# Where four small streams stand in a hand-ordered attention and gate kernel: key-feature exponentials, feature minima, LN2 norms, a memory product

## The chip, the cores and the metric

The kernel runs on one core of a Trainium2 chip. A core has TensorE (matmuls; PE in the profile, its weight loads PEld), VectorE (DVE), ScalarE (ACT), GpSimd (POOL) and SyncE (SP, which here only issues DMAs). Each engine executes its own instructions strictly in the order in which the program issued them, and waits at an instruction until what that needs is there. The metric is the time of one execution on the device, in microseconds; the median of several executions is compared.

## The reference, cut to what matters

A block of 2048 tokens of width 448 goes through attention with a compressive memory and then through a gated layer, each behind a layer norm that is modulated by a vector `c`:

```
mod = silu(c) @ w_mod -> sa, ca, ga, sb, cb, gb
h = LN(x) * (1 + ca) + sa
x = x + ga * attention(h)
h = LN(x) * (1 + cb) + sb
x = x + gb * ((sigmoid(h @ w_gate) * (h @ w_up)) @ w_down)

attention, for each of 4 segments of 512 tokens, 16 heads of width 28:
  phi(t) = t + 1 where t > 0, else exp(t)
  a_dot = softmax(causal(q k^T * scale)) v
  a_mem = (phi(q) M) / (phi(q) z + 1e-6)
  o     = g * a_mem + (1 - g) * a_dot        # g = sigmoid(beta)
  M, z  = M + phi(k)^T v, z + sum(phi(k))
```

So segment s reads a memory that the keys and values of the segments before it have filled; segment 0 reads an empty one.

## The kernel before

**Tiling.** Tokens are cut into 4 segments (s) of 4 tiles of 128. The 16 heads go in 4 chunks (hc) of 4 heads, each head padded from 28 to 32, so that a chunk fills 128 partitions. Attention is done one unit (s, hc) at a time. A unit has three groups g of key blocks (`KB_GROUPS`): block 0; blocks 1 and 3; block 2. I write (s, hc, g) for a group.

**One group** (`logits`, L405): TensorE makes the logits `lg` (L418) in the one PSUM tile for them, ScalarE takes exp into `pT` (L421), GpSimd masks the diagonal blocks (L429). At g = 0 of a later segment `phi` (L363) also starts the query features of the unit.

**`phi`** is an exponential on ScalarE (L365) and, some time later, a pair on VectorE: r = max(x, 0) + 1 (L369) and e = min(e, r) (L370), "the minimum" below. For keys (`mem_k`, L376) a DMA transpose, issued by SP, then brings e into `pk` (L380).

**Per unit besides:** `pv` (L432) multiplies `pT` with the values into `acc` (L443) and divides on VectorE (L449 to L456); `mem_read` (L460) multiplies the query features with the masked memory `rm` (L467) and divides (L470 to L474); `otr` (L485) transposes the unit's result by a DMA on SP (L490). They belong to the unit before the one whose logits are being made.

**Per segment:** `proj_qk` and `proj_v` (L338, L350) make queries, keys (cast by ScalarE or VectorE) and values (cast by ScalarE, L357); `mem_jobs` (L581) starts the four key features and does `mem_update` (L384): 16 matmuls into `dM` (L391), an addition on VectorE (L395, L397), the masking on GpSimd (L400). `wo_tile` (L505) is the output product of one token tile (L502), the addition to x (L512), the statistics of the second layer norm, LN2 (L269, L270), and its 1/std on GpSimd (`rstd`, L273, L274). Some time later `norm_t` (L283) normalizes the tile on VectorE (L277), copies a pad, and issues its DMA transpose into `hT` on SP (L287); when all four are there, `modulate` (L289, L291) scales each of the four chunks of `hT`. Then `gate_up` and `gate_up2` (L527, L546) make gate and up products for two blocks of 128 features (L534, L539, L551), tanh on ScalarE (L542) and the product `fT` on VectorE (L554); `down` (L556) makes one output tile from 14 blocks (L566), adds (L568) and stores it.

**PSUM.** All products but the logits rotate through four buffers (`ps_m`, tag "m"): a product waits until the one four before it has been read out.

**What sets the order.** The kernel issues its instructions in an order that a small planner in the code makes when the kernel is built. It has a clock (`clock`), advanced by `tick` with an assumed cost in ns of each job (a Q or K product 4 * 216, a V or output tile 4 * 190, a group of logits 450, a PV 1000, a memory read 250). `later(ns, fn, tag)` puts work off until the clock has passed its due time; `need(tag)` does all work of a tag at once. `fill` is a queue of jobs; after each group `run_fill` issues jobs for `pace` ns, and what it overran is carried as a (negative) `debt`. In segment 0 pace is 2400; from (s, 1, 0) on it is the cost of what is left, divided by 12. `gate_up2` is issued right behind the next group's logits. PV of the unit before stands in g = 1; where s > 1 it stands already in g = 0 if pace plus debt isn't positive.

The order of `fill` decides when a segment's other work is done. For segments 0 and 1 it is built at L749 to L754, for later ones at L780 to L801.

Of the kernel before, what the change touches and what calls it, by code (L numbers as in the profile page):

```python
# [17 lines left out]
def kernel(  # L18
# [16 lines left out]
    nc = tc.nc  # L35
# [11 lines left out]
    NHC = 4  # L47
# [328 lines left out]
    def mem_k(s, hc):  # L376
        if hc == 0:
            pk_of[s] = pipe.tile([P, NHC, TPS, P], BF16, tag="pk", bufs=1, name="pk")
        pk = pk_of[s]
        phi(kT_of[s][:, hc, :], 3500 if s < 2 else 5000, ("pk", s), lambda e: nc.sync.dma_start_transpose(pk[:, hc, :, :], e[:]))  # L380

    rm_of = {}

    def mem_update(s):  # L384
        need(("pk", s))
        pk = pk_of[s]
        dM = m_f32("dM")
        dMv = dM[:, 0:NHC * 4 * ME].rearrange("p (c h e) -> p c h e", h=4, e=ME)
        for hc in range(NHC):
            for kb in range(TPS):  # L390
                nc.tensor.matmul(dMv[:, hc, :, :], lhsT=pk[:, hc, kb, :],  # L391
                                 rhs=vt_all[s][:, kb, hc * 4:(hc + 1) * 4, 0:ME],
                                 start=(kb == 0), stop=(kb == TPS - 1))
        if s == 0:
            nc.vector.tensor_copy(M_sb[:], dMv)  # L395
        else:
            nc.vector.tensor_tensor(M_sb[:], M_sb[:], dMv, ALU.add)  # L397
        rm = pipe.tile([P, NHC, 4, ME], BF16, tag="rm", bufs=3, name="rm")
        rm_of[s + 1] = rm
        later(800, lambda: nc.gpsimd.tensor_tensor(rm[:], M_sb[:], bmask[:], ALU.mult), ("rm", s + 1))  # L400
# [4 lines left out]
    def logits(s, hc, g):  # L405
# [14 lines left out]
            wid += nq  # L420
        nc.scalar.activation(pT[:, :, w0:w0 + wid], lg[:, :, 0:wid], AF.Exp, scale=scale)  # L421
        if g == 0 and s > 0:
            pq_of[u] = phi(qT[:, hc, :], 3600, ("pq", u))
        for kb in KB_GROUPS[g]:
            later(2600, lambda kb=kb: mask(pT, kb), ("mask", u))

# [82 lines left out]
    def wo_fin(s, t):  # L509
        pw = pw_of.pop(t)  # L510
        xt = x_sb[:, s * TPS + t, :]
        nc.vector.tensor_tensor(xt, pw[:, 0:D], xt, ALU.add)  # L512
        if t == 0:
            ln2_of[s] = LN([x_sb[:, s * TPS + i, :] for i in range(TPS)], ("2", s))
        ln = ln2_of[s]
        ln.stats(t)
        ln.rstd(t, t + 1)
        later(1500, lambda: ln.norm_t(t), ("ln2", s))
        if t == TPS - 1:
            for kc in range(NK):  # L520
                later(6500 + 400 * kc, lambda kc=kc: ln.modulate(kc, 2), ("ln2", s))
# [57 lines left out]
        return jobs  # L579

    def mem_jobs(s):  # L581
        return [(0, lambda: [later((2000 if s < 2 else 2500) * hc, lambda hc=hc: mem_k(s, hc), ("pk", s)) for hc in range(NHC)])] + [(16 * TR, lambda: mem_update(s))]

    def wo_jobs(s):
        return [(4 * MV, lambda t=t: wo_tile(s, t)) for t in range(TPS)]
# [164 lines left out]
    fill.extend(spread(j0[3:6] + sp(late_consts) + j0[6:] + ln1_pe_jobs(1) + [ln1_start(2)]  # L750
                       + j1[:2] + m[0][0:1] + j1[2:4] + [ln1_start(3)] + j1[4:8], early_loads, 1))
    fill.extend(j1[8:] + [(1800, prep_b1)])
    fill.extend(j2[:8] + m[0][1:])
    fill.extend(j2[8:] + j3[:2] + [(2000, prep_b2)] + j3[2:])  # L754

    def cost(jobs):
        return sum(cst for cst, _ in jobs)
# [5 lines left out]
    for s in range(NSEG):  # L763
        for hc in range(NHC):
            prev = (s, hc - 1) if hc else (s - 1, NHC - 1)
            for g in range(3):
# [6 lines left out]
                if prev[0] > 0 and g == 0:  # L773
                    mem_read(*prev)
                    tick(250)
                if prev[0] >= 0 and (g == 1 or g == 0 and s > 1 and pace[0] + debt <= 0) and prev in todo:
                    todo.remove(prev)
                    pv(*prev)
                    tick(1000)
                if s >= 1 and hc == 1 and g == 0:  # L780
# [6 lines left out]
                    for w in wo_jobs(s - 1):  # L787
                        fill.append(w)
                        if tail and s > 1:
                            fill.extend(tail[:2])  # L790
                            tail = tail[2:]
                    fill.extend(tail)
                    if s >= 2:
                        dj = down_jobs(s - 2)
                        if s == 2:
                            gj = gj[:8] + m[2][1:] + gj[8:]
                            dj = dj[:3] + m[2][0:1] + dj[3:]
                        fill.extend(dj[:3] + h2_jobs(s - 1) + dj[3:] + gj)
                    else:
                        fill.extend(h2_jobs(s - 1) + m[1][0:1] + gj[:8] + m[1][1:] + gj[8:])  # L800
                    pace[0] = (cost(fill) - KEEP[s] * GU) / (12 if s < 3 else 9)  # L801
                debt = run_fill(pace[0] + debt)
                if debt > 0:
# [57 lines left out]
```

The softmax here doesn't subtract the row's maximum and nothing guards it: scores larger than these inputs give would overflow.

## Time and profile before

| what | us |
|---|---|
| median of 7 executions | 258.74 (258.03 to 260.01) |
| the profiled execution, its own time | 259.47 |
| its span, first to last instruction | 257.8 |
| TensorE busy | 244.5 |
| VectorE, ScalarE, GpSimd busy | 175.5, 139.8, 75.1 |
| mean granted TensorE clock | 0.993 |

The profile is of one execution. Its views: busy shares of each engine; groups of instructions by line with their mean duration and the idle time in front of them, with the releaser (what ended that idle time); a timeline of one engine (start, duration, engine, line, operation, output and inputs, partitions by elements and type, count; in square brackets the idle time before it and its releaser); windows, with for each engine the busy time and count in a stretch, then the granted clock of TensorE, the busy share of the DMA engines and what they moved. Consecutive instructions of the same kind are merged in a timeline. A wait for several things is put down to the one that came last.

### The profile page before, as it was taken

The numbers are of one execution on the slowest core, as the hardware profiler recorded it, in microseconds if no ns is written. First come the engines' busy times: TensorE is split into PE (matmuls) and PEld (weight loads), VectorE is DVE, ScalarE is ACT, GpSimd is POOL, SyncE is SP. The second block draws the span as 40 slices with busy tenths as digits, with TensorE's granted clock in tenths as the row PEclk, the third lists the DMA queues.
The fourth block names the chain that finished last, engine by engine and source line by source line (L and its number), as shares of the span: only waits on it lengthen the run. The fifth ranks groups of instructions, "written<-read, shape, count | busy, mean of one in ns | idle before, by whom it ended". The sixth has DMA issues, their size and how long they took to land.

```text
span 257.8 us, 5341 instructions
## 1 busy us (share of the span) xinstructions
PE 244.5 (95%) x2083; PEld 114.8 (45%) x2083; DVE 175.5 (68%) x419; ACT 139.8 (54%) x173; POOL 75.1 (29%) x140
## 2 busy tenths in 40 slices
PE   7999997989996979999999999999999999999994
PEld 2534544446533344444544355454353455333453
DVE  6878899585786677988858756895664586544412
ACT  0368898859886696856359666543663200133300
POOL 4368045144344031352502140362020023000000
PEclk9999999999998999999999999999999999999999
DMA  5999996664032024111322410113210015100011
GB/s 155 294 244 260 340 261 125 80 154 83 3 62 45 20 41 64 20 23 20 61 72 47 81 22 1 23 27 94 56 22 3 0 20 119 36 0 0 3 36 36
DMA packets 41168, 19.66 MB, mean 76 GB/s; under 512 B 30008, under 2 KB 40248, under 8 KB 41144
## 3 DMA queue, kind: packets, MB, share of 16 engines
q1 hardware_dynamic: 38408, 17.61, 31.2%
q10 hardware_dynamic: 2736, 1.72, 2.3%
q8 instruction: 16, 0.26, 0.4%
q14 instruction: 8, 0.07, 0.1%
HBM read 10.67 MB, written 1.84 MB: 49 GB/s over the span
## 4 chain that ended last, share of the span: by engine, by line
PE 46%; DVE 10%; issue 2%; POOL 1%; DMA 1%; ACT 1%; SPq 0%; DVEq 0%; POOLq 0%
PE ups L551 12%; PE dps L566 11%; PE gps L534 11%; PE gps L539 4%; PE acc L443 3%; DVE fT L554 2%; PE lg L418 2%; DVE st L269 1%; PE pwo L502 1%; DVE x_sb L512 1%; DVE ot L568 1%; DMA hT<-xn 1%; PE ups L539 1%; PE dM L391 1%; POOL rs L274 1%
## 5 line engine op out<-in xcount | busy, mean ns | idle before, releaser
L421 ACT ACTIVATE pT<-lg 128x2048 bf16<-128x2048 f32 (+1 forms) x48 | 76.7, 1597 | 25.9 <-PE lg L418 21.4
L429 POOL TENSOR_SCALAR_AFFINE_SELECT pT<-pT 128x512 bf16<-128x512 bf16 x64 | 41.7, 668 | 71.2 <-ACT pT L421 71.2
L542 ACT ACTIVATE tt<-gps 128x512 f32<-128x512 f32 x56 | 30.5, 595 | 56.3 <-PE gps L539 56.2
L554 DVE SCALAR_TENSOR_TENSOR fT<-tt,ups 128x512 bf16<-128x512 f32 x56 | 37.1, 686 | 34.1 <-PE ups L551 32.7
L566 PE MATMUL dps<-wd_sb,fT 128*128 128x448 bf16 (+1 forms) x238 | 44.1, 341 | 0.5 <-DVE ot L568 0.5
L534 PE MATMUL gps<-hT,wg_sb 128*128 128x512 bf16 x168 | 42.2, 388 | 0.6 <-ACT vt L357 0.6
L551 PE MATMUL ups<-hT,wu_sb 128*128 128x512 bf16 x168 | 41.1, 381 | 0.0
L566 PEld LDWEIGHTS <-fT 128*128 128x128 bf16 x238 | 22.8, 98 | 19.2 <-issue 0.6
L534 PEld LDWEIGHTS <-wg_sb 128*128 128x128 bf16 x168 | 15.9, 99 | 19.2 <-issue 1.6
L551 PEld LDWEIGHTS <-wu_sb 128*128 128x128 bf16 x168 | 14.1, 97 | 21.6 <-issue 7.7
L443 PE MATMUL acc<-vt,pT 128*128 128x29 bf16 x640 | 18.7, 175 | 3.2 <-POOL pT L429 2.1
L443 PEld LDWEIGHTS <-pT 128*128 128x128 bf16 x640 | 17.7, 96 | 6.4 <-POOL pT L429 2.7
L273 POOL TENSOR_SCALAR rs<-mv 128x1 f32<-128x1 f32 (+2 forms) x21 | 5.4, 259 | 50.8 <-DVE mv L270 50.4
L269 DVE BATCH_NORM_STATS2 st<-x_sb 128x6 f32<-128x448 bf16 x32 | 19.7, 616 | 0.5
L418 PE MATMUL lg<-qT,kT 28*128 28x512 bf16 (+3 forms) x256 | 17.3, 302 | 1.5 <-ACT pT L421 1.5
L539 PE MATMUL ups<-hT,wgu_sb 64*128 64x512 bf16 x56 | 17.9, 383 | 0.7 <-DVE fT L554 0.5
L568 DVE TENSOR_TENSOR ot<-dps,x_sb 128x448 bf16<-128x448 f32 (+1 forms) x17 | 10.1, 594 | 11.6 <-PE dps L566 11.6
L343 PE MATMUL pq<-hT,wq_sb 128*128 128x512 bf16 x64 | 17.0, 380 | 0.9 <-DVE ou L452 0.9
L539 PE MATMUL gps<-hT,wgu_sb 64*128 64x512 bf16 x56 | 17.1, 383 | 0.0
L277 DVE TENSOR_SCALAR xn<-x_sb,mv,rs 128x448 bf16<-128x448 bf16 x32 | 14.2, 461 | 3.8 <-POOL rs L274 3.8
L343 PE MATMUL pq<-hT,wk_sb 128*128 128x512 bf16 x64 | 16.4, 379 | 0.1
L370 DVE TENSOR_TENSOR e<-e,r 128x512 bf16<-128x512 bf16 x24 | 13.8, 573 | 2.4 <-ACT pT L421 0.5
(101 smaller groups left out, 259.9 us busy)
## 6 DMA issues: line engine op xcount, KB each, us to landing
wm<-in_w_mod_dram SPq DMA_DIRECT2D x4, 392.0 KB, 6.9
x_sb<-in_A_x_dram SPq DMA_DIRECT2D x3, 448.0 KB, 6.1
wd_sb<-in_B_w_down_dram SPq DMA_DIRECT2D x3, 448.0 KB, 8.7
wg_sb<-in_B_w_gate_dram SPq DMA_DIRECT2D x3, 448.0 KB, 10.1
wu_sb<-in_B_w_up_dram SPq DMA_DIRECT2D x3, 448.0 KB, 10.6
out_dram<-ot SPq DMA_DIRECT2D x8, 112.0 KB, 1.9
out_dram<-ot ACTq DMA_DIRECT2D x7, 112.0 KB, 1.7
wm<-in_w_mod_dram SPq DMA_DIRECT2D x2, 196.0 KB
```

The lines of the kernel that those rows point to most:

```text
L269: nc.vector.bn_stats(st[:], self.srcs[i])
L343: nc.tensor.matmul(pq[:, 0:L], lhsT=head_cols(w_sb, k, hc), rhs=h[:, k, :], start=(k == 0), stop=(k == NK - 1))
L418: nc.tensor.matmul(lg[:, hs, wid:wid + nq], lhsT=kT[r, hc, kb * P:(kb + 1) * P], rhs=qT[r, hc, kb * P:L], start=True, stop=True, tile_posi ...
L421: nc.scalar.activation(pT[:, :, w0:w0 + wid], lg[:, :, 0:wid], AF.Exp, scale=scale)
L429: nc.gpsimd.affine_select(out=blk, in_=blk, compare_op=ALU.is_ge, fill=0.0, base=0, pattern=[[0, 4], [1, P]], channel_multiplier=-1)
L443: nc.tensor.matmul(accv[:, qb, hs, 0:ME], lhsT=pT[:, hs, c0:c0 + P], rhs=vt[:, kb, hc * 4 + hs, 0:ME], start=(kb == 0), stop=(kb == qb))
L534: nc.tensor.matmul(g[:, 0:L], lhsT=wg_sb[:, k, f], rhs=h[:, k, :], start=(k == 0), stop=False)
L539: nc.tensor.matmul(dst[:, 0:L], lhsT=wgu_sb[r:r + LW, f], rhs=h[r:r + LW, 3, :], start=first, stop=not first, tile_position=(r, 0))
L542: nc.scalar.activation(tt[:], g[:, 0:L], AF.Tanh, scale=0.5)
L551: nc.tensor.matmul(u[:, 0:L], lhsT=wu_sb[:, k, f], rhs=h[:, k, :], start=False, stop=(k == 2))
L554: nc.vector.scalar_tensor_tensor(ft[:], tt[:], 1.0, u[:, 0:L], op0=ALU.add, op1=ALU.mult)
L566: nc.tensor.matmul(dp[:, c], lhsT=fT_of[(s, fc)][:, t * P:(t + 1) * P], rhs=wd_sb[:, fc, c], start=(fc == 0), stop=(fc == NFC - 1))
```

## The change

It moves work and changes delays; every instruction is kept.

- The key features of a segment are no longer put off by a time each, but put in a queue `kq`. Each group that doesn't start query features takes one from it, so that its exponential stands right behind that group's exponential; `mem_update` drains what is left. Their minimum comes 4500 later, instead of 3500 or 5000.
- The minimum of the query features comes 5000 later, instead of 3600.
- The norm of an LN2 tile comes 3200, 2000, 2000 or 1500 behind its statistics (segments 0 to 3), instead of 1500.
- `mem_update` of segment 0 goes behind all of segment 2's projections, V included. The key features of segments 1 and 2 are put in the queue right behind the output tiles of the segment before.
- PV may stand in g = 0 in segment 1 too, for chunks 2 and 3.

```diff
--- before.py
+++ after.py
@@ -377,11 +377,17 @@
         if hc == 0:
             pk_of[s] = pipe.tile([P, NHC, TPS, P], BF16, tag="pk", bufs=1, name="pk")
         pk = pk_of[s]
-        phi(kT_of[s][:, hc, :], 3500 if s < 2 else 5000, ("pk", s), lambda e: nc.sync.dma_start_transpose(pk[:, hc, :, :], e[:]))
+        phi(kT_of[s][:, hc, :], 4500, ("pk", s), lambda e: nc.sync.dma_start_transpose(pk[:, hc, :, :], e[:]))
 
     rm_of = {}
 
+    kq = deque()
+
     def mem_update(s):
+        if kq:
+            print("forced kq", s, len(kq))
+        while kq:
+            kq.popleft()()
         need(("pk", s))
         pk = pk_of[s]
         dM = m_f32("dM")
@@ -420,7 +426,9 @@
             wid += nq
         nc.scalar.activation(pT[:, :, w0:w0 + wid], lg[:, :, 0:wid], AF.Exp, scale=scale)
         if g == 0 and s > 0:
-            pq_of[u] = phi(qT[:, hc, :], 3600, ("pq", u))
+            pq_of[u] = phi(qT[:, hc, :], 5000, ("pq", u))
+        elif kq:
+            kq.popleft()()
         for kb in KB_GROUPS[g]:
             later(2600, lambda kb=kb: mask(pT, kb), ("mask", u))
 
@@ -515,7 +523,7 @@
         ln = ln2_of[s]
         ln.stats(t)
         ln.rstd(t, t + 1)
-        later(1500, lambda: ln.norm_t(t), ("ln2", s))
+        later((3200, 2000, 2000, 1500)[s], lambda: ln.norm_t(t), ("ln2", s))
         if t == TPS - 1:
             for kc in range(NK):
                 later(6500 + 400 * kc, lambda kc=kc: ln.modulate(kc, 2), ("ln2", s))
@@ -579,7 +587,8 @@
         return jobs
 
     def mem_jobs(s):
-        return [(0, lambda: [later((2000 if s < 2 else 2500) * hc, lambda hc=hc: mem_k(s, hc), ("pk", s)) for hc in range(NHC)])] + [(16 * TR, lambda: mem_update(s))]
+        return [(0, lambda: kq.extend([lambda hc=hc: mem_k(s, hc) for hc in range(NHC)])),
+                (16 * TR, lambda: mem_update(s))]
 
     def wo_jobs(s):
         return [(4 * MV, lambda t=t: wo_tile(s, t)) for t in range(TPS)]
@@ -750,8 +759,8 @@
     fill.extend(spread(j0[3:6] + sp(late_consts) + j0[6:] + ln1_pe_jobs(1) + [ln1_start(2)]
                        + j1[:2] + m[0][0:1] + j1[2:4] + [ln1_start(3)] + j1[4:8], early_loads, 1))
     fill.extend(j1[8:] + [(1800, prep_b1)])
-    fill.extend(j2[:8] + m[0][1:])
-    fill.extend(j2[8:] + j3[:2] + [(2000, prep_b2)] + j3[2:])
+    fill.extend(j2[:8])
+    fill.extend(j2[8:] + m[0][1:] + j3[:2] + [(2000, prep_b2)] + j3[2:])
 
     def cost(jobs):
         return sum(cst for cst, _ in jobs)
@@ -773,7 +782,7 @@
                 if prev[0] > 0 and g == 0:
                     mem_read(*prev)
                     tick(250)
-                if prev[0] >= 0 and (g == 1 or g == 0 and s > 1 and pace[0] + debt <= 0) and prev in todo:
+                if prev[0] >= 0 and (g == 1 or g == 0 and s > 0 and (hc > 1 or s > 1) and pace[0] + debt <= 0) and prev in todo:
                     todo.remove(prev)
                     pv(*prev)
                     tick(1000)
@@ -789,15 +798,14 @@
                         if tail and s > 1:
                             fill.extend(tail[:2])
                             tail = tail[2:]
-                    fill.extend(tail)
+                    fill.extend((m[s][0:1] if s < 3 else []) + tail)
                     if s >= 2:
                         dj = down_jobs(s - 2)
                         if s == 2:
                             gj = gj[:8] + m[2][1:] + gj[8:]
-                            dj = dj[:3] + m[2][0:1] + dj[3:]
                         fill.extend(dj[:3] + h2_jobs(s - 1) + dj[3:] + gj)
                     else:
-                        fill.extend(h2_jobs(s - 1) + m[1][0:1] + gj[:8] + m[1][1:] + gj[8:])
+                        fill.extend(h2_jobs(s - 1) + gj[:8] + m[1][1:] + gj[8:])
                     pace[0] = (cost(fill) - KEEP[s] * GU) / (12 if s < 3 else 9)
                 debt = run_fill(pace[0] + debt)
                 if debt > 0:
```

## The prediction

> **What bounds the kernel now.** I read the page's busy shares first, then what TensorE waited for, then the timeline of each engine around each wait. Groups are written (segment, head chunk, group), units (segment, chunk); *planner ns* are issue positions got by adding the costs in the code. They fix each engine's order, not its time.
>
> ```profile
> PE 244.5 (95%) x2083; PEld 114.8 (45%) x2083; DVE 175.5 (68%) x419; ACT 139.8 (54%) x173; POOL 75.1 (29%) x140
> ```
>
> TensorE is busy for 244.5 of 257.8 us. Its work is unchanged, so the change can win only from the 13.3 us between; 5.1 us of these lie in the first 4 and the last 5.8 us (the windows show 2.58 and 2.14 busy there), which it doesn't touch. The other 8.2 sit in a few gaps (start, duration, instruction, idle time before it and its releaser):
>
> ```profile
> 39.67 1.15 PE L443 MATMUL acc<-vt,pT 128*128 128x29 bf16 x40 [1.12 <-DVE kT L348]
> 44.20 1.04 PE L343 MATMUL pq<-hT,wq_sb 128*128 128x512 bf16 x4 [0.88 <-DVE ou L452]
> 54.98 0.39 PE L391 MATMUL dM<-vt,pk 128*128 128x116 bf16 x4 [0.86 <-DMA pk<-e]
> 79.30 1.15 PE L443 MATMUL acc<-vt,pT 128*128 128x29 bf16 x40 [1.76 <-POOL pT L429]
> 81.78 2.74 PE L534 MATMUL gps<-hT,wg_sb 128*128 128x512 bf16 x6 [0.56 <-ACT vt L357]
> 91.82 0.40 PE L418 MATMUL lg<-qT,kT 28*128 28x384 bf16 x8 [1.30 <-ACT pT L421]
> 98.67 0.37 PE L539 MATMUL ups<-hT,wgu_sb 64*128 64x512 bf16 x1 [0.27 <-DVE fT L554]
> ```
>
> All lie before 100 us; after that single gaps are at most 0.35 us. VectorE, GpSimd, ScalarE and SyncE rows show why:
>
> ```profile
> 36.13 0.28 DVE L369 TENSOR_SCALAR r<-kT 128x512 bf16<-128x512 bf16 x1
> 38.96 0.66 DVE L348 CAST kT<-pq 128x512 bf16<-128x512 f32 x1
> 73.12 0.30 DVE L369 TENSOR_SCALAR r<-qT 128x512 bf16<-128x512 bf16 x1
> 74.37 0.62 DVE L512 TENSOR_TENSOR x_sb<-pwo,x_sb 128x448 bf16<-128x448 f32 x1
> 75.95 0.26 POOL L273 TENSOR_SCALAR rs<-mv 128x1 f32<-128x1 f32 x1 [2.68 <-DVE mv L270]
> 76.83 2.44 POOL L429 TENSOR_SCALAR_AFFINE_SELECT pT<-pT 128x512 bf16<-128x512 bf16 x4
> 76.91 0.69 DVE L277 TENSOR_SCALAR xn<-x_sb,mv,rs 128x448 bf16<-128x448 bf16 x1 [0.77 <-POOL rs L274]
> 81.13 1.55 DVE L291 TENSOR_SCALAR hT<-hT,cols 128x512 bf16<-128x512 bf16 x4 [1.98 <-DMA hT<-xn]
> 52.50 1.22 SPq L380 DMA_TRANSPOSE pk<-e  x1
> 89.37 0.63 ACT L365 ACTIVATE e<-kT 128x512 bf16<-128x512 bf16 x1
> 82.00:83.00 1.00, 1.00 (x3) 0.30 (x2) 0.96 (x5) 0.31 (x1) 0.00 (x0) 0.50 0.00 0
> ```
>
> The reader is to see: VectorE runs behind in two places. Output tile 3's product ends at 70.09 and its addition starts only at 74.37; GpSimd stands still for 2.68 us for that tile's statistics with four masks queued behind, and TensorE waits for the masks. The last row (a window; its third number from the end is the granted clock) shows 0.50 right after.
>
> **The change, part by part.** Its instructions are the same in number and kind: 12 key exponentials (632 ns), 24 minima pairs (about 0.73 us start to start), 12 key transposes (1.2 us of SP each), 16 norms. Everything is order.
>
> *1. Segment 0, 36 to 58 us.* The key exponential of chunk 0 moves behind group (0,1,2) and its minimum, now 4500 behind it, from planner 18068 to 21766. So the pair at 36.13 leaves its place ahead of the cast at 38.96: the cast ends about 0.75 earlier and PV (0,1) starts at 38.87 instead of 39.67. Ahead of that PV's division VectorE has one pair instead of three; the wait for the rstd (about 39.7) then rules, `ou` ends near 42.0 instead of 44.14, and the query product starts at 42.5 instead of 44.20: 1.7 us. Of this ScalarE takes some back: the third and fourth key exponentials stand ahead of a V cast and a Q cast there, so (0,2,2) ends on ScalarE at 44.67, and TensorE, ready at 44.24, waits 0.45. Left: 1.45 at (0,3,2).
> The first memory product goes behind four V products and (1,0,0), so it starts near 55.3 and its last four matmuls near 55.95. But the fourth key transpose also moves on SP: past the two w_mod loads and one oT transpose. SP works nearly without a pause from 35.34 to 57.45, and the set ahead of the transpose is then just what stood ahead of the oT issue at 54.93. It is issued between 53.4 (if a 2.52 us issue at 45.95 becomes a normal 1.2) and 54.9 and lands 2.4 later, 55.8 to 57.3: a wait of 0 to 1.3 in place of 0.86. I take 0.6, the middle. Sum of part 1: 1.45 + 0.86 - 0.6 = **1.7** (1.0 to 2.3).
>
> *2. LN2 of segment 0, 66 to 85 us.* (Times in the frame of before.) Norms come 3200 instead of 1500 behind their tile and the query minimum 5000 instead of 3600, so VectorE does, from 71.07: PV (1,0)'s division (1.03), norm 0 (0.51), tile 3's addition and statistics (1.41, to 74.02), norm 1, `ou` (0.36), query minimum (to 75.7), norms 2 and 3 (to 76.64, with no wait for rstd). GpSimd's rstd of tile 3 ends at 74.95 and the three masks that PV needs at 76.85, instead of 79.3. That gap goes, but a new one comes: memory read (1,1) needs the query minimum at 74.55 and gets it at 75.7, **1.2 us**. What is late next is the gate: norm 3 ends at 76.64 instead of 78.1, its transpose is issued at 77.45 (behind norm 2's) instead of 78.15, and by the two landing times seen (2.43 and 2.98) the modulation starts at 79.9 to 80.45 instead of 81.13. One key minimum now falls between modulations 1 and 2 (0.73). So the gate's third product starts at 82.15 and (1,2,2) at about 83.55 instead of 85.06. ScalarE's exponential of chunk 0 moves ahead and costs the casts 0.6, hidden behind that wait. **1.4** (0.4 to 2.3).
> The clock row decides the ends. Full clock would have made the six gate matmuls 1.46 (the row of 86.58) instead of 2.74; some of that was the wait for modulation anyway. If the drop stays I get 0.4 to 0.6, if it goes 1.4 to 2.3; I take it as gone, because the idle time is now split (1.2, then about 0.3) and splits such as 1.12 and 0.88 at 39 and 44 us kept 1.00.
> The Trainium skill ("TensorE: Matmul & The Clock Gate", "What's actually happening") has the gate close after an idle window of about 3.4 us. This trace disagrees: the longest gap was 1.76. By the rule the drop shouldn't have come and nothing could be won from it, and the sum would be some 0.9 lower.
>
> *3. Segment 1, 86 to 100 us.* PV (1,2) goes into g = 0 of chunk 3, because pace + debt is -898 there; it runs (1.0 us) within the 1.30 gap. The key exponential at 89.37 that stood ahead of the exponential ScalarE was late with is gone too. The two key minima and the query minimum at 94.4 to 97.9 that stood ahead of fT shrink to one, so the 0.48 at 98 goes. Replayed with unhindered durations (PV 1.0, gate and up start 1.92, logits 0.33 and 0.22, up 1.31) from 90.47: (2,0,0) at 97.15 instead of 99.57. A key minimum ahead of memory read (1,2) delays PV's division to 94.0, which costs 0.45 in the PSUM ring. **1.95** (0.9 to 2.35). The last key minimum ends at 97.15, lands about 99.7, and memory product 1 wants it at 101.4: hidden, with 1.7 us to spare; beyond that it costs one for one.
>
> *4. Segments 2 and 3.* Key exponentials come earlier; ScalarE is busy 1.2 to 2.9 of 4 us there (128 to 136 us): nothing. The norms that move by 500 go past at most one down product; the last transpose keeps its slot on SP within 0.6 us either way. The query minimum of (3,2) goes from ahead of PV (3,1) to behind an `ot` addition: VectorE gives it at about 180.8, and the memory read wants it at 180.30: minus **0.4** (0 to -0.7).
>
> Sum: 1.7 + 1.4 + 1.95 - 0.4 = 4.65. The profiled execution took 259.47 (span 257.8): it would be 254.8. The median shown is 0.73 lower, 258.74; from there, 254.1.
>
> **Rivals.** (a) *All gaps close*: upper ends, 2.3 + 2.3 + 2.35 - 0 = 6.95, so 251.8. For it: few rows bind twice. Against: the minimum for read (1,1) is late by VectorE's own backlog. 0.12. (b) *The next engine binds*: the key transpose waits on SP, the clock drops again, and ScalarE, busy 3.98 and 3.72 of 4 us in 60 to 68, keeps segment 1 where it is. Then part 1 is worth about 0, parts 2 and 3 are 0.4 and 0.9, less 0.4: 0.9, so 257.8. Against: ScalarE reaches (1,0,1) some 2 us earlier than before, since its exponential (1,0,0) no longer stands behind the memory product. 0.11. (c) *Slower: memory reads wait for the query minimum.* All 12 are issued 1400 later on an in-order VectorE that was 4.3 us behind at 74.37. One mechanism, at the head of each chunk; I find it at two reads. If VectorE is late by a mean of 0.6 at all twelve (half of what I find at (1,1)), that is 7.2 instead of the 1.6 I counted: 5.6 more, so 259.7; at 0.75 it is 9.0, so 261.5. It passes no change at 6.25 us in all and +0.5% at 7.5. Against: most reads come 3 us or more behind their minimum. 0.07. That the change doesn't do what it says (keys left in the queue, drained all at once ahead of a memory product) is excluded by count: each segment has four groups that drain one ahead of its product.
>
> **How the numbers follow.** My forecast, 254.1, has 0.70. Half a percent, 1.3 us, is about what a measurement of this kernel can tell from no change. Faster is the forecast and (a): 0.82; the same is (b): 0.11; slower (c): 0.07. The range is that of the parts: best 251.8, worst 1.0 + 0.4 + 0.9 - 0.7 = 1.6 less, 257.1; stretched to 257.3, where (b) begins. That leaves out 0.18.
>
> **What would show it.** Part 1: no gap ahead of PV (0,1) over 0.5, none ahead of the query product at 42.5; a wait for `pk` under 1.3. Part 2: a new wait of a memory read for `e` near 74, masks no longer awaited, granted clock 1.00 near 80. Part 3: PV directly behind the memory read, no wait for `pT` near 90. Part 4: a wait ahead of a memory read three quarters through. I am wrong if the clock drop stays, if the fourth transpose lands after 57.3, or if reads other than (1,1) and (3,2) wait.

## The result, and the profile after

The changed kernel takes 262.05 us (median of 13 executions, 259.99 to 262.91); the kernel before took 259.26 beside it (34 executions, 258.03 to 261.34). The ratio is 1.0097, with a 95% interval from 1.0073 to 1.0121: **one per cent slower**. 254.1 had been forecast, in a range up to 257.3. The profiled execution took 262.62 (span 260.9). Line numbers behind L380 have moved by 6 to 8: the memory product is L397 now, `acc` L451, the memory read L475, the gate L542.

The busy shares of the changed kernel show that each engine has as many instructions as before; VectorE's take 2.2 us longer:

```profile
PE 245.1 (94%) x2083; PEld 114.7 (44%) x2083; DVE 177.7 (68%) x419; ACT 139.7 (54%) x173; POOL 74.8 (29%) x140
```

What TensorE waited for in it (us in total, times, the longest) is other than before. The masks and the logits' PSUM tile have all but gone from the list, and three others lead it; of these only the first stood there before, with 0.9:

```profile
PE dM L397 <- DMA pk<-e: 2.8, 2, 1.5
PE mem L475 <- DVE e L370: 2.4, 2, 1.6
PE gps L542 <- DVE hT L291: 2.0, 3, 1.1
...
PE acc L451 <- POOL pT L437: 0.3, 1, 0.3
```

TensorE's timeline of the changed kernel at the places that the prediction had named:

```profile
38.96 1.15 PE L451 MATMUL acc<-vt,pT 128*128 128x29 bf16 x40 [0.38 <-DVE kT L348]
42.78 1.02 PE L343 MATMUL pq<-hT,wq_sb 128*128 128x512 bf16 x4 [0.16 <-PE lg L424]
55.34 0.58 PE L397 MATMUL dM<-vt,pk 128*128 128x116 bf16 x8
57.46 0.38 PE L397 MATMUL dM<-vt,pk 128*128 128x116 bf16 x4 [1.53 <-DMA pk<-e]
59.10 0.38 PE L397 MATMUL dM<-vt,pk 128*128 128x116 bf16 x4 [1.26 <-DMA pk<-e]
76.68 0.39 PE L475 MATMUL mem<-rm,e 128*128 128x116 bf16 x4 [1.59 <-DVE e L370]
83.18 0.69 PE L542 MATMUL gps<-hT,wg_sb 128*128 128x512 bf16 x2 [1.11 <-DVE hT L291]
84.55 1.87 PE L542 MATMUL gps<-hT,wg_sb 128*128 128x512 bf16 x4 [0.68 <-DVE hT L291]
92.88 1.16 PE L451 MATMUL acc<-vt,pT 128*128 128x29 bf16 x40
```

The first two rows are the gain of part 1: the gaps of 1.12 and 0.88 are 0.38 and 0.16. The next three are its loss: 2.79 us of waiting for key transposes in place of 0.86. Then the wait of memory read (1,1) for its query minimum, the two gaps of the gate, which waits longer than before, and PV (1,2) directly behind its memory read, as forecast.

Where the time went is seen by comparing, in the two profiled executions, when TensorE starts the same group of logits (after minus before, us):

| up to group | forecast for the stretch | measured for the stretch | sum so far |
|---|---|---|---|
| (0,3,2), start of part 1 | -1.45 | -1.44 | -1.44 |
| (1,0,1), the memory product | -0.25 | +2.11 | +0.67 |
| (1,2,2), LN2 and the gate | -1.4 | +1.59 | +2.26 |
| (2,0,0), the rest of segment 1 | -1.95 | -1.19 | +1.07 |
| the end | +0.4 | +2.07 | +3.14 |

SyncE's timeline of the changed kernel (its records are the issues of DMAs):

```profile
51.09 1.07 SPq L120 DMA_DIRECT2D wm<-in_w_mod_dram  x2
52.24 1.19 SPq L380 DMA_TRANSPOSE pk<-e  x1
53.48 1.30 SPq L498 DMA_TRANSPOSE oT<-ou  x1
54.88 1.22 SPq L380 DMA_TRANSPOSE pk<-e  x1
```

The two `w_mod` loads (392 KB each) now stand ahead of the third key transpose and of the fourth; before, they were issued behind all four, at 53.81. TensorE's wait for the third ended 5.2 us after its issue (57.4 less 52.24) and that for the fourth 4.2 after (59.06 less 54.88). Before, the fourth was issued at 52.50 and TensorE had it by 54.98, 2.5 later.

VectorE's timeline of the changed kernel in the LN2 stage has the four norms (L277, with a pad copy, L281), and the query minimum for read (1,1) between them:

```profile
72.72 0.75 DVE L277 TENSOR_SCALAR xn<-x_sb,mv,rs 128x448 bf16<-128x448 bf16 x1
...
75.01 0.38 DVE L277 TENSOR_SCALAR xn<-x_sb,mv,rs 128x448 bf16<-128x448 bf16 x1
...
76.19 0.42 DVE L370 TENSOR_TENSOR e<-e,r 128x512 bf16<-128x512 bf16 x1
76.54 0.71 DVE L277 TENSOR_SCALAR xn<-x_sb,mv,rs 128x448 bf16<-128x448 bf16 x1
77.28 0.49 DVE L281 COPY xn<-xn 128x64 bf16<-128x64 bf16 x1
77.69 0.77 DVE L277 TENSOR_SCALAR xn<-x_sb,mv,rs 128x448 bf16<-128x448 bf16 x1
...
82.33 1.11 DVE L291 TENSOR_SCALAR hT<-hT,cols 128x512 bf16<-128x512 bf16 x2 [2.33 <-DMA hT<-xn]
```

The same instruction takes 0.38 at 75.01 and about 0.75 in the other three places. GpSimd's rows tell what is beside those three:

```profile
72.71 0.64 POOL L437 TENSOR_SCALAR_AFFINE_SELECT pT<-pT 128x512 bf16<-128x512 bf16 x1
76.29 2.65 POOL L437 TENSOR_SCALAR_AFFINE_SELECT pT<-pT 128x512 bf16<-128x512 bf16 x4
```

And the clock dropped again, as the third number from the end in this window of the changed kernel shows:

```profile
85.00:86.00 1.00, 1.00 (x4) 0.23 (x2) 0.93 (x3) 0.00 (x0) 0.00 (x0) 0.50 0.61 125
```

### The profile page after: what moved, and what is told of

Its sections match the earlier page's. It is cut to its first block, busy times and chain, and to the rows that moved or that the text cites. A ratio compares the mean times of both kernels' runs of the same rounds, so it can differ in the third digit from the quotient of the medians.

```text
span 260.9 us, 5336 instructions
## 1 busy us (share of the span) xinstructions
PE 245.1 (94%) x2083; PEld 114.7 (44%) x2083; DVE 177.7 (68%) x419; ACT 139.7 (54%) x173; POOL 74.8 (29%) x140
## 3 DMA queue, kind: packets, MB, share of 16 engines
q10 hardware_dynamic: 2736, 1.72, 2.4%
## 4 chain that ended last, share of the span: by engine, by line
PE 49%; DVE 12%; DMA 3%; issue 3%; ACT 2%; POOL 1%; SPq 0%; POOLq 0%; DVEq 0%; ACTq 0%
PE ups L559 13%; PE gps L542 12%; PE dps L574 9%; PE gps L547 5%; DMA hT<-xn 3%; PE acc L451 3%; PE lg L424 2%; PE pwo L510 2%; DVE st L269 2%; DVE x_sb L520 2%; DVE fT L562 2%; DVE hT L291 1%; DVE e L370 1%; ACT pT L427 1%; DVE xn L277 1%
## 5 line engine op out<-in xcount | busy, mean ns | idle before, releaser
L542 PE MATMUL gps<-hT,wg_sb 128*128 128x512 bf16 x168 | 42.2, 385 | 2.0 <-DVE hT L291 2.0
L542 PEld LDWEIGHTS <-wg_sb 128*128 128x128 bf16 x168 | 15.8, 98 | 20.9 <-issue 3.0
L451 PE MATMUL acc<-vt,pT 128*128 128x29 bf16 x640 | 18.7, 175 | 1.2 <-DVE t L482 0.5
L451 PEld LDWEIGHTS <-pT 128*128 128x128 bf16 x640 | 17.7, 96 | 4.1 <-issue 2.2
L277 DVE TENSOR_SCALAR xn<-x_sb,mv,rs 128x448 bf16<-128x448 bf16 x32 | 15.4, 502 | 2.8 <-POOL rs L274 2.6
L274 POOL TENSOR_TENSOR rs<-rs,mhalf 128x1 f32<-128x1 f32 (+2 forms) x21 | 14.2, 676 | 1.8
```

The source lines that it names most:

```text
L451: nc.tensor.matmul(accv[:, qb, hs, 0:ME], lhsT=pT[:, hs, c0:c0 + P], rhs=vt[:, kb, hc * 4 + hs, 0:ME], start=(kb == 0), stop=(kb == qb))
L542: nc.tensor.matmul(g[:, 0:L], lhsT=wg_sb[:, k, f], rhs=h[:, k, :], start=(k == 0), stop=False)
```

## The experiments

The theories. **Q**: the key transposes land late since they stand in SP's queue behind the loads (R is its rival in the texts below). **C**: VectorE's norms are slowed by GpSimd's masks beside them, so the gate is late. **V**: the waits of memory reads for query minima are covered by what ends behind them, so the later minimum costs little; **W**: they cost in full. **K**: of the key features, those of segments 1 and 2 cost time on VectorE. (D, N and O are rivals that each text below explains itself; N isn't the same in runs 3 and 10.) Each run has the kernel before beside it, at 259.1 in all three sets.

### 1. The loads on another queue

```diff
-        wm[4] = load_wm((nc.sync,), 4)
+        wm[4] = load_wm((nc.scalar,), 4)
...
-        wm[3] = load_wm((nc.sync,), 3)
+        wm[3] = load_wm((nc.scalar,), 3)
```

> The changed kernel, with the two w_mod loads of the preparation step (392 KB each) issued from ScalarE's queue instead of SyncE's; all else as in the changed kernel. Theory Q (the transposes of the third and fourth key features stand in SyncE's DMA queue behind these 0.78 MB and land late because of the bytes ahead of them, not because they are issued late): the two waits for pk in front of the memory product of segment 0 (1.53 and 1.26 us) fall to at most 0.6 together, and the time falls by about 2.2 us, from 262.05 to about 259.9. Rival R (the minima on VectorE or SyncE's own issue time make the transposes late): the waits stay above 2 us and the time stays within 0.7 us of 262.05.

264.11 us, ratio 1.020 (1.017 to 1.023): slower by 2 us, where 2.2 less had been expected. The wait for `pk` is gone, but another came. ScalarE's timeline in this run, 42 to 50 us:

```profile
43.08 0.32 ACTq L120 DMA_DIRECT2D wm<-in_w_mod_dram  x1
...
47.66 0.32 ACTq L120 DMA_DIRECT2D wm<-in_w_mod_dram  x1
48.03 1.02 ACT L427 ACTIVATE pT<-lg 128x1024 bf16<-128x1024 f32 x1 [4.04 <-DMA hT<-xn]
```

The second load is issued only at 47.66: ScalarE stood still for 4.04 us around it, put down to a transpose of `hT` that SP issues, and TensorE waited 4.07 for the exponential behind. In the trace this load and that transpose signal the same semaphore, and the load goes out 0.02 after the transpose's last signal. All that follows is shifted by that, and the memory product starts only at 62.5; so its wait and the time decide nothing on Q.

The landings do. From issue to landing the key transposes took, in this run and then in the changed kernel (of the four, the three whose landing the trace tells):

```profile
DMA to landing us min/median/max: 4.9/5.0/5.8
DMA to landing us min/median/max: 2.4/2.4/5.2
```

Here SP issues nothing but transposes, and yet all three land late; the first was issued at 42.36, ahead of the first load at 43.08. So a transpose is late while such a load moves, whichever engine issued the load. Of Q, the loads remain, and SP's queue as the reason falls.

### 2. The query minimum at 3600 again, all else as changed

```diff
-            pq_of[u] = phi(qT[:, hc, :], 5000, ("pq", u))
+            pq_of[u] = phi(qT[:, hc, :], 3600, ("pq", u))
```

> The changed kernel with the query minimum put back to 3600 behind its exponential. Theory V (the stage from 66 to 87 us is bound by VectorE's chain up to the modulation of the gate's input; the memory read's wait of 1.59 us lies inside it and costs nothing of its own): the wait of the memory read (1,1) goes, but the gate still starts at 83.0 to 83.4 us in the trace, and what is won is only the 0.8 us in front of memory read (3,2): about 261.2. Rival W (the memory reads' waits are what the change lost): 1.59 + 0.79 = 2.4 us are won, 259.7.

261.28, ratio 1.0099 (1.0068 to 1.013): 0.8 below the change, with intervals that overlap. The waits of TensorE in this run:

```profile
PE acc L451 <- POOL pT L437: 1.9, 2, 1.6
PE gps L542 <- DVE hT L291: 1.6, 2, 1.3
```

The read's wait has gone, and the masks' wait of the kernel before is back, as long (1.6). The gate, which waits for the modulation of `hT`, is as late. That agrees with V: the two waits stand in for each other, and the stage ends by a third. But the granted clock is at 0.50 for 6.8 us here, from 81.0 on, against 3.4 us in the changed kernel, so a part of what the read's wait was worth may have gone there.

### 3. LN2's norms at 1500 again, all else as changed

```diff
-        later((3200, 2000, 2000, 1500)[s], lambda: ln.norm_t(t), ("ln2", s))
+        later(1500, lambda: ln.norm_t(t), ("ln2", s))
```

> The changed kernel with the LN2 norms of all segments put back to 1500 behind the statistics. Theory V with contention (norms that run beside GpSimd's masks take 0.7 us instead of 0.38, so the later norms made VectorE's chain longer): three of the four norms of segment 0 run before the masks and take 0.38 each again, the modulation of the gate's input starts 0.5 to 1.2 us earlier than at 82.33, the time is about 261.2. Rival D (the delay alone is what cost: the whole lateness of the gate, 1.8 us, is the 1700 later norms): the gate starts as in the kernel before but for the 0.5 us that the stage starts later, and the time is 260.2. Rival N (the norms have nothing to do with it): 262.05 within 0.4.

261.61, ratio 1.0098 (1.0065 to 1.0131). In the trace the LN2 stage no longer loses 1.6 us against before but gains 0.3; of that 0.57 at (3,2,0) is given back, and so is what this execution lost ahead of the stage, where the clock fell to 0.50 for 3.4 us from 59.2 on, right behind the waits for `pk`. The median moves by 0.4 only, between what V (261.2) and N (262.05) had. The size stays unclear here; run 10 repeats it without the wait for `pk`.

### 4. The vacant PV slot alone, in the kernel before

```diff
-                if prev[0] >= 0 and (g == 1 or g == 0 and s > 1 and pace[0] + debt <= 0) and prev in todo:
+                if prev[0] >= 0 and (g == 1 or g == 0 and s > 0 and (hc > 1 or s > 1) and pace[0] + debt <= 0) and prev in todo:
```

> The kernel before, with one part of the change: PV may stand in g = 0 in segment 1 for chunks 2 and 3. Theory: PV (1,2), 1.0 us of TensorE, runs inside the wait of 1.30 us at 91 us; the time falls by 0.8 to 1.0 us, to about 258.3. Rival: the gap only moves (the group behind waits for ScalarE as long as before, or the PSUM buffers for VectorE), within 0.3 us of 259.26.

257.16, ratio 0.9938 (0.9915 to 0.996): 1.9 us, twice what was expected. TensorE's timeline of this run shows why a PV there is free: of the gap of 1.30 that stood ahead of the logits at 91.82, all but 0.30 is now filled.

```profile
89.55 1.16 PE L443 MATMUL acc<-vt,pT 128*128 128x29 bf16 x40
91.02 0.40 PE L418 MATMUL lg<-qT,kT 28*128 28x384 bf16 x8 [0.30 <-ACT pT L421]
```

The small waits for `fT` behind it shrank as well.

### 5. The loads behind the key transposes, all else as changed

```diff
-        wm[4] = load_wm((nc.sync,), 4)
...
-        wm[3] = load_wm((nc.sync,), 3)
+        later(6900, load_wm43, "wm43")
...
+    def load_wm43():
+        for j in (4, 3):
+            wm[j] = load_wm((nc.sync,), j)
...
+        need("wm43")
...
-    fill.extend(j2[8:] + m[0][1:] + j3[:2] + [(2000, prep_b2)] + j3[2:])
+    fill.extend(j2[8:] + m[0][1:] + j3[:4] + [(2000, prep_b2)] + j3[4:])
```

`need` stands in `prep_b2`, which uses the loads and is put two jobs later.

> The changed kernel with the two w_mod loads of the preparation step issued on SyncE behind the fourth key transpose of segment 0 instead of ahead of the third, and with the step that uses them put two projection jobs later; all else as in the changed kernel. Theory Q (the third and fourth key transposes land late because 0.78 MB of loads stand ahead of them in SyncE's queue): SyncE issues these two transposes at about the same times as before or 1 us earlier, they land 2.4 us behind their issue, the waits for pk fall from 2.79 to at most 0.6 us, and the time falls by 2.0 to 2.5 us to about 259.8. Rival R (minima or issue time are what is late): waits above 2 us, 262 within 0.7.

258.44, ratio to before 0.9984 (0.9967 to 1.0): 3.6 below the changed kernel. SyncE's timeline in this run, and TensorE's memory product:

```profile
49.41 2.53 SPq L380 DMA_TRANSPOSE pk<-e  x2
51.99 1.26 SPq L498 DMA_TRANSPOSE oT<-ou  x1
53.34 1.22 SPq L380 DMA_TRANSPOSE pk<-e  x1
54.65 1.07 SPq L120 DMA_DIRECT2D wm<-in_w_mod_dram  x2
```

```profile
55.41 1.00 PE L397 MATMUL dM<-vt,pk 128*128 128x116 bf16 x16
```

The 16 matmuls run without a pause. The fourth transpose is issued 1.54 earlier than in the changed kernel, yet its data are there 3.3 us earlier (55.78 and 59.06). From issue to landing the key transposes took, in this run:

```profile
DMA to landing us min/median/max: 2.4/2.4/2.5
```

At (1,0,1) this run is 3.08 ahead of the changed kernel: 2.79 of waits and 0.3 around them. **The loads are what made the transposes late**; that they stood in the same queue isn't needed for it, by run 1. What is left of the change now only equals the kernel before: a gain of 2.4 at (1,0,1) is given back later, 0.6 of it at once, since TensorE now waits for the loads (0.69 at 62.22).

### 6. The memory product behind V, alone, in the kernel before

```diff
-    fill.extend(j2[:8] + m[0][1:])
-    fill.extend(j2[8:] + j3[:2] + [(2000, prep_b2)] + j3[2:])
+    fill.extend(j2[:8])
+    fill.extend(j2[8:] + m[0][1:] + j3[:2] + [(2000, prep_b2)] + j3[2:])
```

> The kernel before, with one part of the change: the first memory product behind all V of segment 2; keys, minima and norms as in the kernel before. Theory: the place is right by itself, and only the later keys of the change spoiled it: the wait of 0.86 us for pk goes, nothing else moves, 0.5 to 0.9 us are won, about 258.4. Rival: the later memory product makes its masking on GpSimd, and so masks or the memory read, late: the same time or slower, 259.1 or more.

258.03, ratio 0.996 (0.9945 to 0.9974): 1.05 faster, and no wait for `pk`. Here the loads come behind all four transposes (53.44), since the key exponentials are as early as before. So it isn't the later memory product that hurts, but the later key features, which fall behind the loads.

### 7. The masks earlier, all else as changed

```diff
-            later(2600, lambda kb=kb: mask(pT, kb), ("mask", u))
+            later(1000, lambda kb=kb: mask(pT, kb), ("mask", u))
```

> The changed kernel, with every diagonal mask issued 1000 instead of 2600 behind its group, so that in the LN2 stage of segment 0 three masks stand ahead of the fourth tile's 1/std on GpSimd and are done before norms 2 and 3. Theory C (those norms took 0.7 to 0.8 us instead of 0.38, their pad copies 0.49 instead of 0.18, because GpSimd's masks ran at the same time, and this made the gate late): norms 2 and 3 take 0.38 each, the gate's input is modulated 1.0 to 1.5 us earlier against the start of the stage, the time falls by about 1.2 to 260.8. Rival O (the order on VectorE alone made it late): modulation no more than 0.3 earlier, 262 within 0.5.

261.71, ratio 1.012 (1.0088 to 1.0153); no gain. VectorE's timeline in this run:

```profile
75.89 0.71 DVE L277 TENSOR_SCALAR xn<-x_sb,mv,rs 128x448 bf16<-128x448 bf16 x1
...
77.14 0.39 DVE L277 TENSOR_SCALAR xn<-x_sb,mv,rs 128x448 bf16<-128x448 bf16 x1
...
81.61 1.18 DVE L291 TENSOR_SCALAR hT<-hT,cols 128x512 bf16<-128x512 bf16 x2 [2.84 <-DMA hT<-xn]
```

Norm 3 isn't slowed by a mask (0.39), but norm 2 is (0.71), and that decides: SP issues norm 2's transpose at 77.25, and norm 3's 1.72 later at 78.97, though its data have been there since 77.74. In the changed kernel that distance is 1.72 too (77.80 and 79.52). The contention had been moved to another norm, not taken away, so the time says nothing for or against C; but the run shows that the fourth transpose is tied to the third. Why by 1.72 is open.

### 8. The parts that gain, together

The PV slot (4), the product behind V (6), the loads behind the transposes (5), and the key features of segment 0 one per group; norms, query minima and the keys of segments 1 and 2 as before.

```diff
-        phi(kT_of[s][:, hc, :], 3500 if s < 2 else 5000, ("pk", s), lambda e: nc.sync.dma_start_transpose(pk[:, hc, :, :], e[:]))
+        phi(kT_of[s][:, hc, :], (4500, 3500, 5000)[s], ("pk", s), lambda e: nc.sync.dma_start_transpose(pk[:, hc, :, :], e[:]))
...
+        elif kq:
+            kq.popleft()()
...
+        if s == 0:
+            return [(0, lambda: kq.extend([lambda hc=hc: mem_k(s, hc) for hc in range(NHC)])), (16 * TR, lambda: mem_update(s))]
```

> The kernel before with the parts of the change that I take for good and one mend: PV in g = 0 in segment 1, key features of segment 0 one per group with their minima 4500 later, the memory product behind V, and the w_mod loads behind the key transposes; query minima, LN2 norms and the keys of segments 1 and 2 as in the kernel before. If the gains add up: 1.9 (PV, as measured) + 1.4 (TensorE's lead at the end of segment 0 in the changed kernel) + 0.9 (the wait for pk) = 4.2 below 259.1, 254.9. If the stage of LN2 or ScalarE takes part of it back: 256 to 257.

255.60 (255.04 to 256.7), ratio 0.9872 (0.985 to 0.9894): the best of all, 3.5 below the kernel before and 6.4 below the changed one, and between the 254.9 of a full sum and the 256 of the other expectation. TensorE's longest wait that is left in it:

```profile
PE acc L449 <- POOL pT L435: 2.1, 2, 1.7
```

The masks' wait (1.75 at 77.23) is the one that the kernel before has at 79.30.

### 9. Masks beside norms, made on purpose

In the kernel before, segment 3 has no masks of its own near its LN2. Two masks on a scratch tile are added behind each 1/std there: extra work, and the output doesn't depend on it.

```diff
+        if s == NSEG - 1:
+            for _ in range(2):
+                nc.gpsimd.affine_select(out=scr[:], in_=scr[:], compare_op=ALU.is_ge, fill=0.0, base=0,
+                                        pattern=[[0, 4], [1, P]], channel_multiplier=-1)
```

> The kernel before, with two more diagonal masks on a scratch tile (128x512, as all masks) behind each 1/std of segment 3's LN2 on GpSimd, where it has no masks otherwise. Theory C (a norm or pad copy, all in SBUF, that runs beside a mask takes up to twice its time; instructions that read PSUM don't): the norms at 208 to 220 us that overlap with a mask take 0.6 to 0.8 us instead of 0.36 to 0.40, while the additions stay at 0.62 and the statistics at 0.63. Rival: all stay as they were, and the 0.7 us norms of the other stages have another cause.

One execution: 264.07. Two of VectorE's norms in this run, each with the addition that follows it, and then GpSimd's masks (each row is a pair; one takes 0.64):

```profile
210.90 0.38 DVE L279 TENSOR_SCALAR xn<-x_sb,mv,rs 128x448 bf16<-128x448 bf16 x1
211.21 0.61 DVE L514 TENSOR_TENSOR x_sb<-pwo,x_sb 128x448 bf16<-128x448 f32 x1
...
212.74 0.69 DVE L279 TENSOR_SCALAR xn<-x_sb,mv,rs 128x448 bf16<-128x448 bf16 x1
213.36 0.61 DVE L514 TENSOR_TENSOR x_sb<-pwo,x_sb 128x448 bf16<-128x448 f32 x1
```

```profile
210.52 1.34 POOL L522 TENSOR_SCALAR_AFFINE_SELECT scr<-scr 128x512 bf16<-128x512 bf16 x2
...
212.67 1.34 POOL L522 TENSOR_SCALAR_AFFINE_SELECT scr<-scr 128x512 bf16<-128x512 bf16 x2
```

Both norms overlap with a mask. The second begins 0.07 into one and takes 0.69, and so do the two that follow it; without a mask the norms of this segment take 0.36 to 0.40 in the kernel before. The first begins 0.38 into a mask, when most of it is over, and takes 0.38. All four end 0.13 behind the end of their mask. The addition, which reads one input from PSUM, takes 0.61 beside a mask, and 0.59 to 0.62 without one in the kernel before. **C's mechanism is shown**, with a limit: a mask slows the norm that begins early in it.

### 10. Run 5 with LN2's norms at 1500

The edit of run 3 on the kernel of run 5.

> The changed kernel with the w_mod loads behind the key transposes (258.44 us), and the LN2 norms back at 1500. Theory N (the later norms are what made the gate of segment 0 late, since norms 2 and 3 went behind tile 3's statistics and beside the masks, on the path to the transposes): the gate starts 1.2 to 2 us earlier against the start of its stage, 256.5. Rival (the norms' lateness is covered, the rest of the stage sets it): within 0.5 of 258.4.

257.73, ratio 0.9944 (0.9923 to 0.9966): 0.7 below run 5, less than expected. VectorE in this run, and a window of TensorE's clock:

```profile
74.46 0.69 DVE L277 TENSOR_SCALAR xn<-x_sb,mv,rs 128x448 bf16<-128x448 bf16 x1 [0.46 <-POOL rs L274]
...
78.32 0.74 DVE L291 TENSOR_SCALAR hT<-hT,cols 128x512 bf16<-128x512 bf16 x2 [1.62 <-DMA hT<-xn]
```

```profile
81.00:82.00 1.00, 1.00 (x5) 0.23 (x3) 0.93 (x3) 0.00 (x0) 0.00 (x0) 1.00 0.64 131
```

Three norms take 0.38 to 0.39 ahead of the four masks; only the last is slow. The fourth transpose is issued at 75.70 instead of 77.21 in run 5 and the modulation starts 1.6 earlier; the clock stays at 1.00, and (1,2,2) is 1.9 ahead of run 5, 0.48 of it already at (1,1,2), ahead of the stage. Only 0.7 of the 1.9 reach the median. A part is that run 5's profile had the drop and most of its executions, by their mean clock, had not: among those at 0.998 or more the medians are 258.30 (8 of run 5) and 257.73 (10 of this run), 0.6 for the norms alone. Another 0.58 is given back at (3,2,0). I didn't trace the rest.

### 11. Run 5 with the query minimum at 3600

The edit of run 2 on the kernel of run 5.

> The changed kernel with the w_mod loads behind the key transposes (258.44 us), and the query minimum back at 3600. Theory V (the wait of memory read (1,1) lies inside a stage that the modulation ends): only the wait of 0.8 in front of memory read (3,2) is won, 257.6 to 258.0. Rival W (both waits are lost time): 1.6 + 0.8 less, 256.0.

258.78 (258.65 without one execution at 261.95), ratio 0.997 (0.9944 to 0.9996): nothing gained on run 5's 258.44. The masks' wait is back at 1.6, as in run 2. V missed by 0.8 and W, which had 256.0, by 2.8. The clock differs: it is at 0.50 for 6.8 us from 77.9 on (3.4 us in run 5's profile), and 2 of the 12 executions have a mean of 0.998 or more, against 8 in run 5; what of the wait's worth went there isn't separated. But the fastest execution took 257.52, so W falls in its size: the waits for query minima are not what the change loses by.

### 12. Run 8 with the change's key features of segments 1 and 2

```diff
-        if s == 0:
+        if s >= 0:
...
-                    fill.extend(tail)
+                    fill.extend((m[s][0:1] if s < 3 else []) + tail)
...
-                            dj = dj[:3] + m[2][0:1] + dj[3:]
...
-                        fill.extend(h2_jobs(s - 1) + m[1][0:1] + gj[:8] + m[1][1:] + gj[8:])
+                        fill.extend(h2_jobs(s - 1) + gj[:8] + m[1][1:] + gj[8:])
```

and 4500 for all minima of keys.

> The combination of 255.6 us, with the change's key features for segments 1 and 2 too: one per group, minimum 4500 later, queued right behind the output tiles. Theory K (for segments 1 and 2 the order is a loss: one minimum, 0.73 us, falls between the modulations of the gate's input, and one in segment 2 ahead of a memory read's division): 0.6 to 1.3 us slower, 256.2 to 256.9. Rival (ScalarE gains from it as in segment 0): 255.6 or less.

256.90, ratio 0.9903 (0.9866 to 0.994): 1.3 above run 8, whose interval this one's just overlaps; in the two profiled executions it is 0.8. VectorE's timeline of this run ahead of (3,0,1):

```profile
142.79 0.28 DVE L369 TENSOR_SCALAR r<-kT 128x512 bf16<-128x512 bf16 x1
143.11 0.89 DVE L370 TENSOR_TENSOR e<-e,r 128x512 bf16<-128x512 bf16 x1
143.93 0.16 DVE L476 SCALAR_TENSOR_TENSOR r<-mem,coef 128x16 f32<-128x16 f32 x1
```

A key minimum of segment 2 stands directly ahead of a memory read's division and takes 0.89, beside a mask that GpSimd begins at 143.09 (the last key minimum of run 8, with no mask beside it and another instruction behind, takes 0.43). The division ends at 145.03, 1.3 later than in run 8, 0.2 of which was there at (3,0,0). From (3,0,0) to (3,0,1) this run loses 0.6 on run 8, and the changed kernel, with the same three instructions at 147.74, loses 0.6 on the kernel before. K holds in its amount and place. One link isn't shown: the up product that starts 0.47 late there is by the profile released by ScalarE's tanh of the gate, before the division ends, so the way from the division to TensorE stays open.

## Why the prediction was wrong

**Part 1: the order was right, a landing time was wrong.** Up to (0,3,2) the replay gave -1.45, and -1.44 was measured. That it agrees so closely is partly luck: the query product started at 42.78 instead of 42.5, and the wait of 0.45 on ScalarE behind it didn't come. The step that failed is "It is issued between 53.4 [...] and 54.9 and lands 2.4 later, 55.8 to 57.3: a wait of 0 to 1.3". The issue was at 54.88, within its bounds. The 2.4 was a row from a place where no load was moving; with two loads issued shortly before, it was 4.2, and 5.2 for the third transpose, which I had not put behind the loads at all. So the term was 2.79 instead of 0.6, with what is around it 2.4 us of the error; run 5, which moves only the loads (and what uses them), gains 3.08 in the trace.

**Part 2: norms sized by a row without masks.** The failed step is "norm 0 (0.51)" and "norms 2 and 3 (to 76.64, with no wait for rstd)". With their copies, norms 0, 2 and 3 took 0.88, 1.15 and 1.21 up to the next start, since all three now fall beside masks. The row of 76.91 that I showed, 0.69, was such a norm, and I read past it. The rest of the path in numbers, in the frame of before (0.67 less than after): norm 2 with its copy ends at 77.1 instead of 76.13, 0.97 late; norm 3's transpose is issued 1.72 behind norm 2's instead of the 1.31 I used, 0.41 more; so it goes out at 78.85 instead of 77.45. By the landing times that I had, which held (2.81 from issue to modulation), the modulation comes at 81.66, later than in the kernel before (81.13). With that, "I take it as gone" failed too: TensorE's gaps of 1.59, 0.48, 1.11 and 0.68 were followed by a clock of 0.50 for 3.4 us. A forecast of -1.4 became +1.6: 3.0 of the error, its largest piece. How this divides between the norms and the clock is settled only in part: in the traces, undoing the norms' delay gains 1.9 with the clock's share in it, in medians 0.7, among executions without a drop 0.6. And the clock isn't all of the loss: executions with a mean clock of 0.997 or more took 260.2 (two of the changed kernel) and 258.5 (ten of the kernel before), so about 1.6 of the 2.8 us is lost at full clock too.

The new wait of read (1,1) was forecast at 1.2 and came at 1.59. Taking it away wins nothing that can be told (runs 2 and 11), since the masks then end as late as they did and the stage ends at the modulation anyhow; that the clock was lower for longer in both runs is a second reason that they don't rule out.

**Part 3: right in kind.** PV in the vacant slot was seen directly behind the memory read, and alone is worth 1.9 (run 4; 1.5 of it between (1,2,2) and (2,0,0) in the trace). In the changed kernel the stretch gained 1.19 instead of 1.95. The new rows that stand against it are `ups` waits on VectorE (0.57 at 96.87).

**Part 4: two places missed.** -0.4 was forecast for read (3,2), and 0.38 was lost there. Not seen was the key minimum of segment 2 ahead of a memory read's division, with a loss of 0.6 there (run 12 has it too, and run 8 hasn't). The step was "Key exponentials come earlier; ScalarE is busy 1.2 to 2.9 of 4 us there (128 to 136 us): nothing": I had checked ScalarE, and not VectorE, where the minimum follows. Another 0.8 is lost in small pieces behind 190 us, about half of it idle, and 0.3 near 117; these weren't traced.

**The rivals.** Rival (b), "the key transpose waits on SP, the clock drops again", named the two places where most was lost, but not how: the transpose didn't wait on SP, it landed late. And it priced part 1 at about 0; it was +0.67. Rival (c) had the sign but not the cause. That the forecast kept a slower end was right; its 7.5 us of waits for query minima were not what led there: 2.4 us came, at the two reads that had been found. Two of the three marks that I had set came: the clock drop stayed, and the fourth transpose landed after 57.3.

**What a page says of it.** The Trainium skill ("SBUF — State Buffer", section "Who interferes with whom") has VectorE and GpSimd share a pair of SBUF ports that one of them holds for a whole instruction; operations from SBUF to SBUF such as the norm and the copy can be caught by it, those with at most one SBUF input outside such modes not. This case agrees in the direction: norm 0.38 to 0.69, copy 0.18 to 0.49, addition from PSUM 0.61 to 0.61. It also fits a wait until the mask lets go: in run 9 all four norms end 0.13 behind their mask, whether they began 0.07 or 0.38 into it, and only those that began early are longer. How long a mask holds the ports no run here shows directly.

## What to carry to other kernels

A DMA's time from issue to landing belongs to what else is moving then: when a step moves a small transfer past a large one, price it by a row from behind a large one, or move the large one out of its way in time; another queue wasn't enough here. The duration of a VectorE instruction belongs to what GpSimd does beside it: take it from a row with the same neighbour at the same distance, and ask what a shift of a stream puts it beside. And when an instruction is moved, follow its successors on each later engine; the one that I had checked was free, the next one wasn't.

## What the runs showed of the hardware

- A DMA transpose that SP issued behind two plain loads of 392 KB each in the same queue was awaited until 4.2 and 5.2 us after its issue; with the loads issued by ScalarE instead, such transposes landed after 4.9 to 5.8 (run 1); with no load moving, after 2.4 to 2.5 (once 3.2, at 100.36 in the changed kernel). Why a load holds transposes up is open.
- Issues of key transposes followed each other in 1.31 us. Those of `hT` at LN2 came 1.29 (run 2) and 1.72 apart where the data were there before; why these differ is open.
- A plain load issued by ScalarE was held up, and ScalarE with it for 4.04 us, until a transpose of SP's that signals the same semaphore had landed (run 1).
- VectorE's instructions from SBUF to SBUF grow beside a mask of GpSimd: norm 0.38 to 0.69 (up to 0.77), copy of 64 columns 0.18 to 0.49, key minimum 0.43 up to 0.89. A norm that began 0.38 into a mask of 0.64 kept its 0.38 (run 9).
- The granted clock halves for 3.4 us (6.8 in runs 2 and 11) after gaps that are all under 1.8 us, and not each time: in run 10 gaps of 1.6 and 1.2 kept 1.00 in the profile. Of the changed kernel's 13 executions the two with a mean clock of 0.998 or more took 259.99 and 260.33, the others, at 0.993 or less, 261.5 to 262.9. Of the kernel before's 53 beside the experiments, 10 had 0.997 or more, with a median of 258.5 against 259.2.
